# Four small moves in the opening of a fused FFT and SoLU kernel: the mean row of w_out, its last piece, the first down product, and the loads of the second pair

## The chip, the cores, the metric

The kernel runs on one core of a Trainium2 chip. The metric is device time in microseconds (us), the median of several executions. The profile's span (first to last instruction) is some 2 us shorter than the device time of the same execution.

## The reference

```python
# x: (8, 3136, 256); w_in: (256, 1024); w_out: (1024, 256); g_ln: (1024,)
X = np.fft.fft(np.fft.fft(x, axis=1), axis=2).real          # then (25088, 256)
h = X @ w_in
e = np.exp(h - h.max(-1, keepdims=True))
solu = h * e / (e.sum(-1, keepdims=True) + 1e-9)
ln = (solu - solu.mean(-1)) / np.sqrt(solu.var(-1) + 1e-6) * g_ln
out = ln @ w_out
```

## The kernel before

The eight batches are handled as four pairs. A pair's rows are transformed along the sequence in two stages (`transform1`, `transform2`, with a trip through DRAM between them), and each row block of the result is a *unit*: an "up" product with w_in (the feature transform is folded into it), the softmax-like middle, and a "down" product with w_out. Unit 0 has one half, the others two (signs 0 and 1). Subtracting the mean over features is done once, on w_out: its mean row is subtracted (`centre`), and `weight_sums` prepares four differences of blocks for a seven-product multiplication. The weights come as 64-bit floats and are converted by integer operations (`exponent`, `confine`, `narrow`).

```python
def confine(unit, here=False):              # limit the exponent
    if here:                                # two operations on VectorE
        bits(unit, unit, -896.0, ALU.add, 0.0, ALU.max)
        bits(unit, unit, 255.0, ALU.min, 2.0 ** 23, ALU.mult)
        return
    ...                                     # else three on ScalarE
def centre(self):
    cs = result(0)[:, 0:D]
    for c in range(KF):
        nc.tensor.matmul(cs, ones, Wo[:, c, :], start=(c == 0), stop=(c == KF - 1))
    nc.scalar.mul(out=wbar, in_=cs, mul=1.0 / FF)
    nc.vector.tensor_tensor(out=Wo, in0=Wo, in1=wbar.unsqueeze(1).to_broadcast([P, KF, D]), op=ALU.subtract)
def weight_sums():                          # four on GpSimd, each 128x512
    for j, (a, b) in enumerate(((B12, B11), (B22, Ws[:, 0]), (B22, B12), (B21, Ws[:, 1]))):
        nc.gpsimd.tensor_tensor(out=Ws[:, j], in0=a, in1=b, op=ALU.subtract)
def ahead(pr, i):                           # loads, mirror sum (GpSimd), fold (VectorE) of a later pair
    if i == (pr.p - 1) * NK:
        load(pr, 0); load(pr, 1)            # each: one DMA of SyncE, one gather of GpSimd
    ...
# The opening (cuts marked; engines in comments)
...
for i in range(1, 3): weights.narrow_out(i)             # VectorE
for t in units[:2]: take2(t, transform2(...)); spread(t)  # spread: r <- q, 512 bytes
confine(weights.units[-1])                              # ScalarE
for c in (...): keep(first, c, ...)                     # 2.6 MB to DRAM, SyncE's queue
weights.load_table(1)
...
def begin(i):                                           # starts unit i
    enter(i)
    even(cur, up(cur, 0))                               # TensorE, then VectorE: ev = h0 + w_mid * r
    cur.odd = up(cur, 1)
    second_transform(i + 2)                             # TensorE, copied by ScalarE
begin(0)
for i in range(whole + 1):                              # whole = 4
    if prv: turn_whole(prv)                             # TensorE transposes of unit i-1, into four banks
    for s in cur.signs: join(cur, s)                    # VectorE
    if prv: ...                                         # VectorE copies two of the four banks
    for s in cur.signs: expo(cur, s)                    # ScalarE
    if i == whole: ps_o = down(units[0], 0)             # TensorE, 16 matmuls
    if i == 0: weights.narrow_out(3)                    # VectorE
    for s in cur.signs:
        product(cur, s)                                 # VectorE: u = h * u, two SBUF inputs
        if i < whole and s == 0: square(cur, s)         # ScalarE
    if i == 1: weights.centre(); weight_sums()
    if i < whole:
        begin(i + 1)
        if 1 in cur.signs: square(cur, 1)
        stats(cur); power(cur)                          # ScalarE, then GpSimd: rs
    else:
        ...
        scale(units[0], 0, ps_o)
    if i == 0: turn(first, 1, nc.sync)
    other_pairs(i, ahead)
```

Each engine runs its own instructions in the order of the program.

## Time and profile before

| | before |
|---|---|
| median of 6 runs | 1178.57 us (1176.2 to 1179.94) |
| span of the profiled run | 1174.4 us |
| TensorE / VectorE / ScalarE / GpSimd busy | 1132.6 / 1005.7 / 762.4 / 598.2 us |

A row of the timeline gives start, length, engine, source line, operation, the tile written and those read, shapes and count; in brackets, how long the engine idled before it and who ended the wait. A releaser is inferred, so where the engine named had been done for long, another one was meant. The times of the "evens" (line 244, one for each unit) serve as a ruler for the opening; the prediction shows them.

**A measure for what follows.** The code is the same up to the first narrowing of w_out, and from TensorE's first `transform1` of the second pair on. Between them lies all that the diff touches. I call the time from the start of the one to the start of the other *the stretch*: 45.20 to 111.77 us before, so 66.57.

### The profile page before, as it was taken

How to read it: one execution, taken by the hardware profiler on the slowest of the kernel's cores; microseconds unless marked ns; L12 is line 12 of the kernel's file. 1: busy time of each engine (PE TensorE's matmuls, PEld its weight loads, DVE VectorE, ACT ScalarE, POOL GpSimd, SP SyncE). 2: the span in 40 equal slices, each digit the busy share in tenths (PEclk: the TensorE clock that was granted, in tenths of full speed). 3: DMA queues.
4: the chain of work that ended last, by engine and by line, in shares of the span. 5: the costliest groups of instructions: out<-in, count | busy, mean ns of one | idle time of the engine just before them, and what ended most of it. 6: DMA issues, size and time to landing. Idle time of an engine off the chain costs nothing. (4 is left out here: it accounts for less than half of the span.)

```text
span 1174.4 us, 18577 instructions
## 1 busy us (share of the span) xinstructions
PE 1132.6 (96%) x5850; PEld 881.2 (75%) x5850; DVE 1005.7 (86%) x1376; ACT 762.4 (65%) x1841; POOL 598.2 (51%) x558
## 2 busy tenths in 40 slices
PE   2988999999999999999999999999999999999997
PEld 1556787777877787877877777778777787778787
DVE  7789999998878999998879999999887898888870
ACT  4577666757756766767656666676666676677651
POOL 3036666563465566563556666554544334433444
PEclk9999999999999999999999999999999999999999
DMA  9672998865988998865879898865775565745553
GB/s 243 196 186 71 180 183 180 176 141 127 180 185 167 182 167 186 176 141 135 176 146 188 176 188 183 172 146 133 153 154 135 135 152 125 154 108 137 130 116 109
DMA packets 458465, 185.55 MB, mean 158 GB/s; under 512 B 425750, under 2 KB 440350, under 8 KB 458368
## 3 DMA queue, kind: packets, MB, share of 16 engines
q1 hardware_dynamic: 444608, 146.22, 60.4%
q0 software_dynamic: 13760, 38.16, 12.4%
q8 instruction: 47, 0.77, 0.3%
q14 instruction: 50, 0.41, 0.1%
HBM read 44.78 MB, written 38.80 MB: 71 GB/s over the span
## 5 line engine op out<-in xcount | busy, mean ns | idle before, releaser
L443 PE MATMUL ps_m<-Wo,uT 128*128 128x256 f32 x1632 | 369.2, 380 | 3.1 <-ACT uT L321 2.1
L238 PE MATMUL ps_h<-Wi,q 128*128 128x512 f32 x800 | 360.8, 593 | 3.0 <-DVE nmax L252 2.1
L443 PEld LDWEIGHTS ps_m<-Wo,uT 128*128 128x128 f32 x1632 | 314.2, 196 | 33.8 <-ACT uT L321 2.4
L268 DVE SCALAR_TENSOR_TENSOR u<-h,u 128x1024 f32<-128x1024 f32 x196 | 266.1, 1366 | 50.5 <-ACT u L261 36.1
L238 PEld LDWEIGHTS ps_h<-Wi,q 128*128 128x128 f32 x800 | 145.9, 190 | 149.9 <-issue 140.0
L275 ACT ACTIVATE h<-u,usum 128x1024 f32<-128x1024 f32 x196 | 224.4, 1145 | 34.3 <-DVE u L268 33.0
L354 POOL TENSOR_TENSOR S<-uT 128x512 f32<-128x512 f32 x94 | 130.4, 1387 | 208.5 <-issue 138.7
L261 ACT ACTIVATE u<-h,neg 128x1024 f32<-128x1024 f32 x196 | 225.3, 1150 | 6.4
L304 DVE STREAM_TRANSPOSE v<-u 128x1024 f32<-128x1024 f32 x192 | 227.8, 1226 | 0.1
L291 POOL TENSOR_TENSOR rs<-v,neg_half 128x2 f32<-128x2 f32 (+1 forms) x100 | 71.7, 717 | 251.8 <-ACT v L284 251.7
L252 DVE CUSTOM_DVE_ANT_0 h<-ev,ps_h 128x1024 f32<-128x1024 f32 x100 | 122.2, 1222 | 33.3 <-PE ps_h L238 23.5
L244 DVE SCALAR_TENSOR_TENSOR ev<-w_mid,r,ps_h 128x1024 f32<-128x1024 f32 x100 | 126.7, 1267 | 25.6 <-PE ps_h L238 20.6
L359 PE MATMUL ps_m<-Ws,S 128*128 128x128 f32 x1128 | 141.5, 275 | 1.8 <-ACT ot L390 1.8
L216 ACT COPY q<-ps_m 128x256 f32<-128x256 f32 x100 | 36.8, 368 | 159.4 <-PE ps_m L210 155.9
L359 PEld LDWEIGHTS ps_m<-Ws,S 128*128 128x128 f32 x1128 | 133.6, 192 | 2.7 <-issue 1.6
L252 DVE CUSTOM_DVE_ANT_0 h<-h,ps_h 128x1024 f32<-128x1024 f32 x96 | 117.3, 1221 | 13.8
L454 POOL DMA_INDIRECT out_dram<-ot,idx x96 | 100.8, 1050 | 30.7 <-issue 18.7
L359 PE MATMUL ps_m<-Wo,uT 128*128 128x128 f32 x752 | 104.2, 282 | 0.1
L182 PE MATMUL ps_m<-y,F 98*100 98x258 f32 (+3 forms) x288 | 73.4, 390 | 24.7 <-DVE y L130 21.8
L210 PEld LDWEIGHTS ps_m<-T,g 128*128 128x128 f32 x400 | 60.2, 191 | 49.1 <-issue 41.7
L359 PEld LDWEIGHTS ps_m<-Wo,uT 128*128 128x128 f32 x752 | 96.1, 196 | 0.9 <-issue 0.5
L259 ACT ACTIVATE neg<-nmax 128x1 f32<-128x1 f32 x196 | 38.4, 196 | 81.5 <-DVE nmax L252 73.6
(87 smaller groups left out, 1186.7 us busy)
## 6 DMA issues: line engine op xcount, KB each, us to landing
uT<-v SPq DMA_DIRECT2D x752, 128.0 KB
out_dram<-ot SPq DMA_DIRECT2D x100, 128.0 KB
g<-zd POOLq DMA_DIRECT2D x72, 160.0 KB, 5.6
xa<-in_x_dram SPq DMA_DIRECT2D x28, 392.0 KB
zd<-z SPq DMA_DIRECT2D x24, 400.0 KB
raw_in<-in_moe_w_in_dram SPq DMA_DIRECT2D x4, 512.0 KB
raw_out<-in_moe_w_out_dram SPq DMA_DIRECT2D x2, 1024.0 KB
r<-q SPq DMA_DIRECT2D x100, 0.5 KB
```

Source lines behind the costliest of these rows:

```text
L182: nc.tensor.matmul(o[..., cs], F[:, 2 * t + h, :], i[..., cs], start=first, stop=True, skip_group_check=True)
L238: nc.tensor.matmul(ps[:, fs], t.q[:, c * P : (c + 1) * P], Wi[:, c, fs], start=True, stop=True)
L244: nc.vector.scalar_tensor_tensor(out=t.ev, in0=w_mid, scalar=t.r, in1=ps, op0=ALU.mult, op1=ALU.add)
L252: nc.vector.tensor_tensor_reduce(out=t.h[s], in0=t.h[0] if s else t.ev, in1=t.odd, scale=1.0 if s else -0.5, scalar=-3.0e38, op0=ALU.add, ...
L261: nc.scalar.activation(out=t.u[s], in_=t.h[s], func=ACT.Exp, bias=t.neg[:, s : s + 1], accum_out=t.esum[:, s : s + 1])
L268: nc.vector.scalar_tensor_tensor(out=t.u[s], in0=t.h[s], scalar=1.0, in1=t.u[s], op0=ALU.mult, op1=ALU.mult, accum_out=t.usum[:, s : s + 1])
L275: nc.scalar.activation(out=t.h[s], in_=t.u[s], func=ACT.Square, bias=t.usum[:, s : s + 1], scale=-float(FF), accum_out=t.ssq[:, s : s + 1])
L304: nc.vector.transpose(out=t.batch.v[:, t.w, :, o], in_=t.u[s])
L354: nc.gpsimd.tensor_tensor(out=t.S[:, j], in0=a, in1=b, op=op)
L359: nc.tensor.matmul(o, a[:, c], b[:, c], start=start and c == 0, stop=c == n - 1, skip_group_check=True)
L443: nc.tensor.matmul(ps, uT[:, c, :, s], Wo[:, c, :], start=(c == 0), stop=(c == KF - 1))
L454: dma = nc.gpsimd.indirect_dma_start(out=out, out_offset=bass.IndirectOffsetOnAxis(ap=idx[:, i : i + 1], axis=0), in_=t.ot[s], in_offset=None)
```

## The change

It wants VectorE out of the way in the opening, where VectorE sets the pace: the mean row is subtracted by GpSimd; the last piece of w_out is converted together with the others, its exponent confined by GpSimd; the first down product (`down(units[0], 0)`) goes into a gap of TensorE one step sooner; and the loads of the second pair are issued two steps later, out of the way of the small transfer r.

```diff
--- before.py
+++ after.py
@@ -492,13 +492,13 @@
         bits(unit, raw[:, 1 : 2 * NW : 2], 20, ALU.logical_shift_right, 0x7FF, ALU.bitwise_and)
         return unit
 
-    def confine(unit, here=False):
+    def confine(unit, engine=None):
 
         if unit is None:
             return
-        if here:
-            bits(unit, unit, -896.0, ALU.add, 0.0, ALU.max)
-            bits(unit, unit, 255.0, ALU.min, 2.0 ** 23, ALU.mult)
+        if engine:
+            engine.tensor_scalar(out=unit, in0=unit, scalar1=-896.0, scalar2=0.0, op0=ALU.add, op1=ALU.max)
+            engine.tensor_scalar(out=unit, in0=unit, scalar1=255.0, scalar2=2.0 ** 23, op0=ALU.min, op1=ALU.mult)
             return
 
         u = unit.bitcast(FP32)
@@ -606,7 +606,7 @@
             for c in range(KF):
                 nc.tensor.matmul(cs, ones, Wo[:, c, :], start=(c == 0), stop=(c == KF - 1))
             nc.scalar.mul(out=wbar, in_=cs, mul=1.0 / FF)
-            nc.vector.tensor_tensor(out=Wo, in0=Wo, in1=wbar.unsqueeze(1).to_broadcast([P, KF, D]), op=ALU.subtract)
+            nc.gpsimd.tensor_tensor(out=Wo, in0=Wo, in1=wbar.unsqueeze(1).to_broadcast([P, KF, D]), op=ALU.subtract)
 
 
 
@@ -616,7 +616,7 @@
 
     def ahead(pr, i):
 
-        if i == (pr.p - 1) * NK:
+        if i == max((pr.p - 1) * NK, 2):
             load(pr, 0)
             load(pr, 1)
         for c in range(NC):
@@ -701,21 +701,21 @@
         turn(first, 0, nc.sync, 0, 2)
         turn(first, 0, nc.gpsimd, 2, KG)
 
-        confine(weights.units[0], True)
+        confine(weights.units[0], nc.vector)
         for i in range(1, 3):
             confine(weights.units[i])
         weights.product_in(1)
         weights.narrow_out(0)
         weights.exponent_out(3)
+        confine(weights.units[-1], nc.gpsimd)
         weights.product_in(2)
-        for i in range(1, 3):
+        for i in range(1, 4):
             weights.narrow_out(i)
 
         units = [Unit(p, k1) for p in range(NP) for k1 in range(NK)]
         for t in units[:2]:
             take2(t, transform2(pairs[0], t.k1))
             spread(t)
-        confine(weights.units[-1])
         for c in (2, 3, 0, 1, 4, 5, 6, 7):
             keep(first, c, slice(4 * KG, ZR))
         weights.load_table(1)
@@ -739,6 +739,9 @@
             cur = units[i]
             enter(i)
             even(cur, up(cur, 0))
+            if i == whole:
+
+                scale(units[0], 0, down(units[0], 0, result(1)[:, 0:D]))
             cur.odd = up(cur, 1)
             second_transform(i + 2)
 
@@ -761,11 +764,6 @@
                     nc.vector.tensor_copy(out=o, in_=ps)
             for s in cur.signs:
                 expo(cur, s)
-            if i == whole:
-                ps_o = down(units[0], 0)
-            if i == 0:
-
-                weights.narrow_out(3)
             for s in cur.signs:
                 product(cur, s)
                 if i < whole and s == 0:
@@ -786,7 +784,6 @@
                     turn_blocks(cur, s)
                 stats(cur)
                 power(cur)
-                scale(units[0], 0, ps_o)
             if i == 0:
                 turn(first, 1, nc.sync)
             other_pairs(i, ahead)
```

## The prediction

> **What bounds the kernel now.** I began with the page: span 1174.4 us, TensorE 1132.6 us busy, VectorE 1005.7. The table of busy time by stretch (columns: stretch, length, then busy us and, in brackets, instructions of TensorE, weight load, VectorE, ScalarE and GpSimd, granted clock, DMA share, GB/s) tells which engine holds which stage:
>
> ```profile
> 60.00:80.00 20.00, 17.10 (x72) 10.68 (x72) 17.57 (x26) 14.08 (x33) 8.07 (x8) 1.00 0.96 226
> 80.00:100.00 20.00, 16.72 (x75) 10.76 (x74) 19.37 (x29) 18.04 (x42) 5.21 (x6) 1.00 0.12 29
> 120.00:140.00 20.00, 20.00 (x107) 15.86 (x106) 18.50 (x25) 13.72 (x37) 13.08 (x14) 1.00 0.90 166
> 200.00:300.00 100.00, 100.00 (x537) 79.45 (x536) 91.71 (x122) 69.64 (x174) 50.83 (x47) 1.00 0.69 152
> ```
>
> From about 112 us TensorE has no idle worth naming. It does the same work before and after, so the change can pay only by how much sooner that full stretch begins. Before it, VectorE sets the pace: 19.37 of 20 us between 80 and 100. All parts of the diff lie there. The chain of waits that ended last covers the final 3 us and says nothing of it, so I read the timeline of the opening. One step is VectorE's even (L244), two joins (L252), sometimes two PSUM copies (L761), two products (L268). The evens stand at 58.13, 64.73, 75.29, 82.72, 90.20 and 101.22 us. The step from 64.73 to 75.29 is the odd one, 10.6 us where its neighbours take 7.4:
>
> ```profile
> 70.65 1.23 DVE L268 SCALAR_TENSOR_TENSOR u<-h,u 128x1024 f32<-128x1024 f32 x1
> 72.09 2.29 DVE L609 TENSOR_TENSOR Wo<-Wo,wbar 128x2048 f32<-128x2048 f32 x1 [0.21 <-ACT wbar L608]
> 74.47 1.28 POOL L342 TENSOR_TENSOR Ws<-Wo 128x512 f32<-128x512 f32 x1 [4.33 <-DVE Wo L609]
> 75.29 1.28 DVE L244 SCALAR_TENSOR_TENSOR ev<-w_mid,r,ps_h 128x1024 f32<-128x1024 f32 x1 [0.91 <-DMA r<-q]
> 80.44 1.24 DVE L268 SCALAR_TENSOR_TENSOR u<-h,u 128x1024 f32<-128x1024 f32 x1
> 82.72 1.30 DVE L244 SCALAR_TENSOR_TENSOR ev<-w_mid,r,ps_h 128x1024 f32<-128x1024 f32 x1
> ```
>
> See the subtraction (2.29), 0.21 ahead of it for wbar, and 0.91 behind it for a 512-byte transfer, r of unit 2. GpSimd's four weight sums run from 74.47 to 79.5, and the products of unit 2 start only at 80.44, so they miss each other.
>
> **What the Trainium skill says.** "GPSIMD Engine Reference", Performance versus the Vector engine, lists a two-input add of 2048 fp32 columns at 2293 ns on VectorE and 4497 on GpSimd. The trace agrees on VectorE (2.29 us); GpSimd's own points here are 1.28 us for 512 columns and 2.37 for 1020, a slope of 2.15 ns per column, so 2048 columns make 4.6 us (estimate). The same page, Engine selection, calls one-input GpSimd work roughly line-rate; no row here shows one on 512 columns. "SBUF — State Buffer", SBUF: two separate sides, says a VectorE op with two SBUF inputs and a GpSimd op that reads SBUF exclude each other for a whole instruction. The trace agrees: products take 1.23 us alone but, beside GpSimd's S sums in the step at 101 us,
>
> ```profile
> 105.11 1.04 POOL L354 TENSOR_TENSOR S<-uT 128x512 f32<-128x512 f32 x1
> 105.44 1.80 DVE L268 SCALAR_TENSOR_TENSOR u<-h,u 128x1024 f32<-128x1024 f32 x1 [0.17 <-ACT u L261]
> 106.11 2.29 POOL L354 TENSOR_TENSOR S<-uT,S 128x512 f32<-128x512 f32 x1
> 107.17 2.31 DVE L268 SCALAR_TENSOR_TENSOR u<-h,u 128x1024 f32<-128x1024 f32 x1
> ```
>
> they alternate: 1.80 and 2.31. Even and join read one operand from PSUM, and at 74.5 to 79.5 they ran beside the weight sums at 1.28 and 1.22, unharmed. "DMA: Bandwidth & Descriptors", Queues, rings and completion order, says each DMA engine takes a ring in order and alternates between rings. The wait for r fits: it is issued at 68.05 behind large transfers of its own queue, while GpSimd's two x gathers (issued 67.80 and 69.17, some 0.39 MB each) share the engines from another.
>
> **The change, part by part.**
>
> *Last piece of w_out.* ScalarE loses three conversions (3 x 0.72, 56.6 to 58.9), and nothing waited for ScalarE there. VectorE's four-stage narrowing (0.42 + 0.69 + 0.75 + 0.88 = 2.74) moves from 60.94 to 56.05, before the first even. VectorE idled 2.08 us there (the row names ScalarE; the matmuls of h at 56.16 to 58.0 are the real release). So the first even goes from 58.13 to 56.05 + 2.74 = 58.8. The first product comes 4.1 us after it (even 1.28, join 1.22, maximum 0.1, then 1.5 for negation and exponential), at 62.9 instead of 63.59: gain 0.7. Against it: the two new GpSimd ops, some 0.7 each (estimate from the line-rate remark plus dispatch), start near 53 when GpSimd has issued its gather (50.56 to 52.9), beside narrowing ops with two SBUF inputs; lock turns can cost VectorE 0 to 1.4. Net between +0.7 and -0.7; I take 0.
>
> *Mean subtraction.* VectorE loses 2.29 and 0.21, and is ready for the third even at 72.0. GpSimd runs it from 72.2 to 76.8, the weight sums to 81.8. Nothing needs them before the first seven-product step near 101; TensorE's first down product, near 85, needs Wo alone.
>
> *x loads of the second pair, two steps later.* This takes 0.78 MB of gather out of r's way. The transfers queued ahead of r had about 0.48 MB left when the gathers began near 69 (windows of bytes moved: 2.8 MB of 3.28 MB gone). At about 220 GB/s that ends at 71.1 alone and 73.4 shared. r was seen at 75.2, so 1.8 us go to completion: r lands near 72.9 now. The third even thus goes from 75.29 to about 73.0: **gain 2.3**, not the 3.4 of removed VectorE time plus waits, because r takes over as limit. The loads, now issued around 85 to 88, land by 91 to 93; GpSimd's mirror sum stood at 93.25 behind rs, so they stay hidden.
>
> *What is paid back.* The products of unit 2 now start at 73.0 + 5.15 = 78.15, inside the weight sums (76.8 to 81.8). By the alternation above, the first waits out the sum in flight (0.6 to 1.2) and the second a whole one (1.2): **loss 1.2 to 2.4, I take 1.8**. So the fourth even goes from 82.72 to about 82.2.
>
> *First down product.* TensorE's 16 matmuls (3.73 us) leave the place where they waited 2.14 for their bank and push the next up product:
>
> ```profile
> 93.58 3.73 PE L443 MATMUL ps_m<-Wo,uT 128*128 128x256 f32 x16 [2.14 <-ACT uT L321]
> 97.14 3.60 PE L238 MATMUL ps_h<-Wi,q 128*128 128x512 f32 x8
> 108.92 2.02 PE L359 MATMUL ps_m<-Ws,S 128*128 128x128 f32 x16 [0.80 <-ACT ot L390]
> 111.77 1.11 PE L182 MATMUL ps_m<-y,F 98*100 98x258 f32 x4 [0.83 <-ACT q L216]
> ```
>
> TensorE gets about 3 us ahead at 97. But it stops again at 108.9 and 111.8 for ScalarE, which follows VectorE's products, so most of this becomes waiting. In its new place, between the halves of unit 4's up product at 85, it ends near 89 and the second half near 90.7, while the join that reads it starts near 91: a tight fit, no loss expected.
>
> *Sum.* VectorE's chain 0 + 2.3 - 1.8 = 0.5 us sooner, which reaches the end one for one; some 0.5 more if the alternation is milder or TensorE's lead saves one of the two waits.
>
> **The rivals.** (1) *The lock does not bite* and the products keep 1.23 us: gain 2.3 to 3, about 1175. For it: small ordering changes can let VectorE's products pass together. Against: the rows at 105 and 107. (2) *The lock bites at all places*, narrowing and products, and the displaced up product delays the join: 0.5 to 1.5 us slower, about 1179. For it: GpSimd carries 10 us of work between 72 and 82, nearly all of one step. (3) *r is not helped* by moving the loads, being bound by its own queue: the third even stays near 74.5 to 75 and products and sums overlap less; about equal to before. Against: only 0.48 MB stood ahead of it when the gathers came. (4) *TensorE is the bound in the opening too*, and the moved down product pays its 2.14 us in full: about 1175. Against: its 0.80 and 0.83 us of waits after it.
>
> **Range and chances.** The runs before lie between 1176.2 and 1179.94, so the clock itself adds about 1.5 either way. Path gain 0.5 to 1, some weight on rival 1 and 4 (each about 1 in 4) over 2 (1 in 5): predicted 1176.6, range 1173.4 to 1179.6. Two per cent is 23.6 us; all that the change touches on VectorE's path is under 7 us, so leaving the band of 2% needs an accident such as a mistimed load: 1 in 100 each way.
>
> **What would show it.** The third even at about 73.0 with r as its releaser; the subtraction on GpSimd at 4.6 us; the products of unit 2 above 1.23, summing to about 4.2; the fourth even near 82; TensorE waiting longer before 108 and full from about 111. The prediction is wrong if the products stay at 1.23 (then faster), if the third even comes at 72 (r no limit), if GpSimd's subtraction takes well over 4.6 us and runs into the products itself, if the mirror sum waits for the late loads, or if TensorE's stretch after 112 is not as full as its busy share says.

## The result

The changed kernel took 1181.82 us (1180.67 to 1183.5, 6 runs) against 1178.57: ratio 1.003, 95% interval 1.0017 to 1.0043. A ratio is the mean time of one kernel's fast runs over that of the other's of the same rounds, so not quite the ratio of the medians. It is within 2%, as forecast, but slower, and outside the range.

The profiled run has a span of 1181.6 us. Of the 7.2 us over the 1174.4 of before, 3.1 came before the first narrowing, where no instruction differs, and 1.2 after the stretch. The stretch itself went from 66.57 to 69.47 us: **2.90 longer**, which agrees with the 3.25 between the medians. The evens share it out (us from the first narrowing):

| | before | changed | difference |
|---|---|---|---|
| second even | 19.53 | 19.86 | +0.33 |
| third even | 30.09 | 28.33 | -1.76 |
| third to fourth | 7.43 | 9.44 | +2.01 |
| fourth to fifth | 7.48 | 7.45 | -0.03 |
| fifth to sixth | 11.02 | 13.76 | +2.74 |
| sixth to the end of the stretch | 10.55 | 10.49 | -0.06 |
| stretch | 66.57 | 69.47 | +2.90 |

(The stretch is the sum of the rows from the third even down.) The timeline of the changed kernel, first part, shows the GpSimd work and what it does to VectorE:

```profile
58.12 1.96 POOL L501 TENSOR_SCALAR scratch<-scratch 128x512 int32<-128x512 int32 x1
...
75.55 4.56 POOL L609 TENSOR_TENSOR Wo<-Wo,wbar 128x2048 f32<-128x2048 f32 x1 [4.60 <-ACT wbar L608]
...
76.61 1.28 DVE L244 SCALAR_TENSOR_TENSOR ev<-w_mid,r,ps_h 128x1024 f32<-128x1024 f32 x1 [1.31 <-DMA r<-q]
...
82.08 1.83 DVE L268 SCALAR_TENSOR_TENSOR u<-h,u 128x1024 f32<-128x1024 f32 x1 [0.22 <-ACT u L261]
...
82.78 2.26 POOL L342 TENSOR_TENSOR Ws<-Wo 128x512 f32<-128x512 f32 x1
...
83.83 2.29 DVE L268 SCALAR_TENSOR_TENSOR u<-h,u 128x1024 f32<-128x1024 f32 x1
```

The second of the two new confining operations takes 1.96 us (the first 2.04); a narrowing operation beside it (L522, at 58.21) is stretched to 1.10 (0.75 before). The subtraction takes 4.56. The third even comes sooner, held by r as predicted. Then the products of unit 2 take 1.83 and 2.29 us, turn about with the weight sums, which grow to 2.26. Before, these two products took 1.24 us each, at 80.44 and 81.58. The second part holds the surprise:

```profile
86.05 1.27 DVE L244 SCALAR_TENSOR_TENSOR ev<-w_mid,r,ps_h 128x1024 f32<-128x1024 f32 x1
...
86.19 1.97 PE L316 MATMUL ps_m<-ident,u 128*128 128x128 f32 x8 [1.13 <-DVE u L268]
...
87.94 2.71 PE L238 MATMUL ps_h<-Wi,q 128*128 128x512 f32 x4
...
90.49 3.62 PE L443 MATMUL ps_m<-Wo,uT 128*128 128x256 f32 x16
...
93.94 1.88 PE L238 MATMUL ps_h<-Wi,q 128*128 128x512 f32 x4
...
95.95 1.22 DVE L252 CUSTOM_DVE_ANT_0 h<-ev,ps_h 128x1024 f32<-128x1024 f32 x1 [1.17 <-PE ps_h L238]
...
96.30 0.37 ACT L216 COPY q<-ps_m 128x256 f32<-128x256 f32 x1 [1.62 <-PE ps_m L210]
...
97.85 1.22 DVE L252 CUSTOM_DVE_ANT_0 h<-h,ps_h 128x1024 f32<-128x1024 f32 x1 [0.66 <-ACT h L275]
...
100.92 1.81 DVE L268 SCALAR_TENSOR_TENSOR u<-h,u 128x1024 f32<-128x1024 f32 x1 [0.65 <-ACT u L261]
...
114.91 2.02 PE L359 MATMUL ps_m<-Ws,S 128*128 128x128 f32 x16 [0.69 <-ACT ot L390]
```

Read it downward. TensorE's transposes (L316) wait 1.13 for the second, lengthened product, and so does the fourth even; the eight of them take 1.97 us (1.09 in e10, below). The first half of unit 4's up product (L238) takes 2.71 us for four matmuls. The down product (L443) starts only at 90.49, 4.44 us after the fourth even at 86.05, and the second half of the up product stands behind it. So the first join of unit 4 (the L252 at 95.95) waits 1.17 for TensorE. The copy of the next transform (L216 at 96.30) comes late as well, and ScalarE's square behind it; the second join waits 0.66 for that square, because it takes over the buffer that the square uses, and the first product 0.65 for the exponential. In the last row TensorE still stops for ScalarE (0.69, and again 0.82 at 117.75), as before. The 3 us by which TensorE had run ahead became idle time, and the delay of VectorE went to the end.

### The profile page after: what moved, and what is told of

Read it like the earlier page. It is cut to its first block, busy times and chain, and to the rows that moved or that the text cites.

```text
span 1181.6 us, 18579 instructions
## 1 busy us (share of the span) xinstructions
PE 1136.4 (96%) x5850; PEld 884.1 (75%) x5850; DVE 1007.9 (85%) x1375; ACT 760.5 (64%) x1838; POOL 608.9 (52%) x561
## 5 line engine op out<-in xcount | busy, mean ns | idle before, releaser
L443 PE MATMUL ps_m<-Wo,uT 128*128 128x256 f32 x1632 | 369.1, 380 | 0.9 <-ACT q L216 0.9
L238 PE MATMUL ps_h<-Wi,q 128*128 128x512 f32 x800 | 362.3, 595 | 2.2 <-DVE nmax L252 1.1
L443 PEld LDWEIGHTS ps_m<-Wo,uT 128*128 128x128 f32 x1632 | 314.3, 196 | 31.9 <-ACT q L216 1.3
L268 DVE SCALAR_TENSOR_TENSOR u<-h,u 128x1024 f32<-128x1024 f32 x196 | 268.9, 1380 | 52.9 <-ACT u L261 41.8
L238 PEld LDWEIGHTS ps_h<-Wi,q 128*128 128x128 f32 x800 | 146.6, 191 | 149.2 <-issue 139.9
L252 DVE CUSTOM_DVE_ANT_0 h<-ev,ps_h 128x1024 f32<-128x1024 f32 x100 | 122.1, 1221 | 34.8 <-PE ps_h L238 24.3
L216 ACT COPY q<-ps_m 128x256 f32<-128x256 f32 x100 | 36.8, 368 | 163.2 <-PE ps_m L210 159.7
L252 DVE CUSTOM_DVE_ANT_0 h<-h,ps_h 128x1024 f32<-128x1024 f32 x96 | 117.2, 1221 | 14.3 <-ACT h L275 0.7
```

The source lines that it names most:

```text
L238: nc.tensor.matmul(ps[:, fs], t.q[:, c * P : (c + 1) * P], Wi[:, c, fs], start=True, stop=True)
L252: nc.vector.tensor_tensor_reduce(out=t.h[s], in0=t.h[0] if s else t.ev, in1=t.odd, scale=1.0 if s else -0.5, scalar=-3.0e38, op0=ALU.add, ...
L268: nc.vector.scalar_tensor_tensor(out=t.u[s], in0=t.h[s], scalar=1.0, in1=t.u[s], op0=ALU.mult, op1=ALU.mult, accum_out=t.usum[:, s : s + 1])
L443: nc.tensor.matmul(ps, uT[:, c, :, s], Wo[:, c, :], start=(c == 0), stop=(c == KF - 1))
```

## The experiments

All outputs are right. Times of evens are counted from the first narrowing; all columns but the last two are from the one profile of each run. Each ratio is to the runs of the kernel before in the same rounds; their medians were 1177.83 to 1178.95.

| run | third even | 3rd to 4th | 4th to 5th | 5th to 6th | stretch | median, us | ratio to before, 95% |
|---|---|---|---|---|---|---|---|
| before | 30.09 | 7.43 | 7.48 | 11.02 | 66.57 | 1178.57 | |
| changed | 28.33 | 9.44 | 7.45 | 13.76 | 69.47 | 1181.82 | 1.0030 (1.0017 to 1.0043) |
| changed again (e14) | 27.88 | 10.42 | 7.45 | 13.76 | 70.01 | 1180.40 | 1.0021 (1.0011 to 1.0031) |
| e1 down product back | 28.38 | 9.02 | 7.45 | 11.05 | 66.43 | 1179.93 | 1.0011 (0.9994 to 1.0028) |
| e2 down product alone | 29.11 | 7.43 | 8.22 | 12.84 | 68.13 | 1180.34 | 1.0007 (0.9990 to 1.0025) |
| e3 subtraction alone | 29.91 | 8.78 | 7.45 | 11.02 | 67.70 | 1179.01 | 1.0000 (0.9983 to 1.0018) |
| e4 late loads alone | 29.10 | 7.44 | 7.45 | 11.06 | 65.57 | 1177.02 | 0.9986 (0.9968 to 1.0004) |
| e5 last piece alone | 29.36 | 7.45 | 7.45 | 11.01 | 65.81 | 1178.61 | 0.9999 (0.9986 to 1.0013) |
| e6 same, confined by ScalarE | 33.29 | 7.44 | 7.45 | 11.01 | 69.73 | 1181.65 | 1.0032 (1.0021 to 1.0042) |
| e7 changed, sums spaced | 28.76 | 7.46 | 7.73 | 13.42 | 67.88 | 1180.16 | 1.0012 (1.0002 to 1.0021) |
| e10 changed, scaling later | 28.36 | 9.62 | 7.45 | 13.69 | 69.63 | 1181.32 | 1.0027 (1.0018 to 1.0036) |
| e13 changed, sums held back | 28.32 | 7.59 | 7.60 | 12.40 | 66.41 | 1178.37 | 1.0005 (0.9994 to 1.0016) |
| e11 a new version | 26.67 | 9.32 | 7.58 | 12.98 | 67.07 | 1177.89 | 1.0001 (0.9988 to 1.0013) |
| e12 e11 with the down product moved | 26.67 | 9.31 | 7.60 | 12.43 | 66.51 | 1179.32 | 1.0007 (0.9999 to 1.0015) |
| e15 e11, loads one step sooner | 26.70 | 9.32 | 7.58 | 11.01 | 65.13 | 1176.73 | 0.9994 (0.9983 to 1.0004) |
| e17 late loads and down product | 29.10 | 7.44 | 7.45 | 12.46 | 66.95 | 1178.76 | 1.0008 (0.9999 to 1.0017) |

The theory after reading the trace (D): the displaced down product costs the 2.7 us. The main rival (L): the lock between GpSimd and VectorE costs them.

### One part undone, one part alone

e1 puts the down product and its scaling back:

```diff
-            if i == whole:
-                scale(units[0], 0, down(units[0], 0, result(1)[:, 0:D]))      # in begin()
+            if i == whole:
+                ps_o = down(units[0], 0)                                      # behind the exponentials
...
+                scale(units[0], 0, ps_o)                                      # at the end of step 4
```

> The changed kernel with the first down product and its scaling put back to where they were; the other three parts stay. Theory D (the displaced down product costs the time: in the changed kernel's trace the span from the fifth to the sixth even is 13.76 us against 11.02 before): that span returns to 11.0 to 11.3 us and the time falls 2.5 to 3 us below the changed kernel, to within 0.8 us of the kernel before (ratio 0.9995 to 1.0007). Rival L (the shared lock between GpSimd and VectorE, in the narrowing and in the products, costs it): the kernel stays 2.5 us or more slower than before (ratio 1.002 or above).

The span from the fifth to the sixth even returns to 11.05, and the stretch to 66.43, 0.14 less than before. By the trace, D holds for this span. By the median the kernel is within noise of before, so the ratio alone would have decided little.

e2 is the diff's down product alone on the kernel before (the same lines, the other way round).

> The kernel before with the down product moved and nothing else. Theory D: the join of unit 4 waits about 1.2 us for TensorE, the next join and product 0.5 to 0.7 each for ScalarE, the span from the fifth to the sixth even is 13 to 13.8 us, and the time is 2 to 3 us above before (ratio 1.0017 to 1.0026). Rival L: no GpSimd work is added, so the ratio is within 0.0006 of 1. A third view, that the cost needs the other parts' shift of the step, would give something between.

The span is 12.84, somewhat below the 13 expected, and the step ahead of it is 0.74 longer too. TensorE's row of that kernel shows why the second is not the down product's doing:

```profile
84.27 0.68 PE L210 MATMUL ps_m<-T,g 128*128 128x128 f32 x4 [1.74 <-DMA xa<-in_x_dram]
```

The transform at 84.27 waited 1.74 us for gathered rows. (Some releaser names such as `xa` stand for a transfer of the same queue.) So the down product was late here too (at 88.26, 4.35 us after the fourth even at 83.91), but for another reason than in the changed kernel. e2 doesn't separate its place from a late TensorE; e17 was made for that.

e3 and e4 are one line each:

```diff
-            nc.vector.tensor_tensor(out=Wo, in0=Wo, in1=wbar...     # e3
+            nc.gpsimd.tensor_tensor(out=Wo, in0=Wo, in1=wbar...
-        if i == (pr.p - 1) * NK:                                    # e4
+        if i == max((pr.p - 1) * NK, 2):
```

> The kernel before with the mean row subtracted by GpSimd and nothing else. My account: r still lands near 75.2 us, so the third even gains nothing; the subtraction takes 4.5 to 4.6 us, the products of unit 2 collide with one or two of the weight sums and lose 1 to 2 us together; ratio 1.0005 to 1.0017. If removing VectorE work pays by itself, the third even comes 2 us or more sooner and the ratio is 0.9985 or below.

> The kernel before with the loads of the second pair issued two steps later and nothing else. My account: r lands by about 73, before VectorE has done the subtraction, so the 0.9 us wait of the third even goes and nothing else moves; ratio 0.999 to 0.9996. If the late loads hurt (mirror sum waiting for them, then the fold), the step from the fifth to the sixth even grows and the ratio is above 1.

With the subtraction alone, the third even waits 3.23 us for r, so removing 2.29 us from VectorE gained 0.18 there; the products of unit 2 took 1.45 and 2.29, the step grew by 1.35, and the stretch by 1.13, as expected. The ratio (1.0000) is too wide to confirm it. With the late loads alone the wait for r is gone, and the stretch is 1.00 shorter, as expected; the ratio (0.9986) leans that way and isn't clear of 1. Nor is one profile proof: in e2 and e5, with the loads in their old place, the third even didn't wait for r either (29.11 and 29.36).

e5 and e6 convert the last piece of w_out in one go, with the exponent confined by GpSimd or by ScalarE:

```diff
+        confine(weights.units[-1], nc.gpsimd)      # e5; e6: without the engine, so by ScalarE
         weights.product_in(2)
-        for i in range(1, 3):
+        for i in range(1, 4):
             weights.narrow_out(i)
```

> The kernel before with the last piece of w_out converted in one go, its exponent confined by GpSimd, and nothing else. From the trace of the changed kernel: each GpSimd operation takes about 2 us instead of the 0.7 I assumed, VectorE's narrowing beside it is stretched by about 1.2 us, so the first even comes 1.6 us later than before (counted from the first narrowing of w_out) and the first product, because the narrowing is out of the way, only 0.3 to 0.4 later or equal; the stretch from the first narrowing to TensorE's first transform of the second pair stays within 0.5 us of 66.57. Rival: this part hurts by itself, and the stretch is 1 us or more longer.

> As the one before, but the exponent is confined by ScalarE as the other pieces are, so GpSimd does nothing there. If the lock is what stretched the narrowing, the stretched rows return to 0.88, 0.42 and 0.75 us, the first even comes at 58.8 to 59.2 on the clock of before and the first product 0.3 to 0.7 us sooner than before. If the narrowing rows stay long, it was not the lock.

In e5 GpSimd's operations took 2.01 and 1.96 us, the first even came at 14.44 (12.93 before) and the first product 0.25 later. The stretch nevertheless is 0.76 shorter, since the 0.91 wait for r is missing in this profile: r's landing varies from run to run. In e6 the stretched narrowing rows are 0.88, 0.42 and 0.74 again, so it was GpSimd's work beside it, as the lock would have it. But the first product gained only 0.14, and the third even waited 4.23 us for r, which nobody expected; the median is 3.4 us above before, so this is no accident of one profile. In e6 the `keep` transfers ahead of r start 0.9 us later against the first narrowing, while GpSimd's gathers come at the same time (22.5 against 22.6), so more stands ahead of r when the gathers join in. That fits, but no run with e6 and late loads was made, so this cause stays argued.

### The lock, taken out of the changed kernel

e7 spreads the four weight sums out, with one after the subtraction, two after the power of step 2, and one after that of step 3:

```diff
-                weight_sums()
+                weight_sums((0,))
...
                 power(cur)
+                if i in (2, 3):
+                    weight_sums((1, 2) if i == 2 else (3,))
```

> The changed kernel with GpSimd's four weight sums spread out: one right after the subtraction, two after the power of step 2, one after that of step 3, so that they miss the products. If the lock costs the changed kernel its gain in this step, the products of unit 2 return to 1.23 us each, and the span from the third to the fourth even returns from 9.44 to 7.4 to 7.9 us. If the span stays at 9 us or more, the products are not what lengthens it. The down product's cost, by my account, stays: the span from the fifth to the sixth even 12.8 to 13.8 us.

Timeline of e7:

```profile
79.93 1.21 DVE L268 SCALAR_TENSOR_TENSOR u<-h,u 128x1024 f32<-128x1024 f32 x1
...
95.40 2.34 POOL L137 TENSOR_TENSOR xa<-xa,xb 98x1020 f32<-98x1020 f32 x1
...
95.80 3.03 DVE L268 SCALAR_TENSOR_TENSOR u<-h,u 128x1024 f32<-128x1024 f32 x1 [0.62 <-ACT u L261]
```

The products of unit 2 are back at 1.21 and 1.22 (the second at 81.07), and the span from the third to the fourth even at 7.46. The 2.0 us were the lock. In the last two rows the same lock strikes elsewhere: the fourth sum pushes the mirror sum (L137) into the first product of unit 4, which takes 3.03. So the 13.42 of this run can't be charged to the down product.

e13 holds all four sums back behind the products of unit 2, with a tiny GpSimd operation that reads their sums:

```diff
+        gate = small.tile([P, 2], FP32, tag="gate", name="gate", bufs=1)
+        nc.gpsimd.tensor_tensor(out=gate, in0=t.usum, in1=neg_half, op=ALU.mult)    # first in weight_sums(t)
...
                     square(cur, 1)
+                if i == 2:
+                    weight_sums(cur)
                 stats(cur)
```

> The changed kernel with its weight sums held back in the same way and nothing else. The lock as cause of the late TensorE: products of unit 2 at 1.23 us, the span from the third to the fourth even 7.4 to 7.7 us (9.44 in the changed kernel), the transposes of that step no longer wait for the products, the down product begins 3.2 to 3.7 us after the fourth even (4.44), the span from the fifth to the sixth even 11.0 to 12 us (13.76), the stretch 65 to 66.5 us. If the down product costs by its place alone, the span from the fifth to the sixth even stays above 12.8.

The products take 1.21 and 1.23, and the down product begins 3.15 us after the fourth even (85.81 and 82.66) instead of 4.44. The stretch is 66.41. But the span from the fifth to the sixth even is 12.40, above the 11 to 12 that the lock alone would leave. So 1.36 us of the 2.74 left in this run, and 1.38 stayed with the down product's place. That the 1.36 were the lock's doing doesn't follow, for a second thing differs: in the changed kernel the granted clock fell just ahead of the down product, and here it held. e10, next, tells the two apart.

### The down product's place

e10 leaves the down product and moves only its scaling behind ScalarE's second square and statistics:

```diff
-                scale(units[0], 0, down(units[0], 0, result(1)[:, 0:D]))
+                units[0].ps = down(units[0], 0, result(1)[:, 0:D])
...
                 power(cur)
+                if i + 1 == whole:
+                    scale(units[0], 0, units[0].ps)
```

> The changed kernel with the down product where it is, but its scaling on ScalarE put behind the second square and the statistics of that step. If ScalarE's wait for the down product's result (0.48 us in the changed kernel) is what delays the joins, the span from the fifth to the sixth even falls from 13.76 to below 12 us. If TensorE's order does it (the second half of the up product and the next transform stand behind the down product, and ScalarE's copy of that transform stands ahead of its square), at most 0.6 us comes back.

The span is 13.69 against 13.76, but its rows are not those of the changed kernel:

```profile
83.17 1.27 DVE L244 SCALAR_TENSOR_TENSOR ev<-w_mid,r,ps_h 128x1024 f32<-128x1024 f32 x1
...
83.30 1.09 PE L316 MATMUL ps_m<-ident,u 128*128 128x128 f32 x8 [1.13 <-DVE u L268]
...
84.49 1.98 PE L238 MATMUL ps_h<-Wi,q 128*128 128x512 f32 x4
...
86.31 3.62 PE L443 MATMUL ps_m<-Wo,uT 128*128 128x256 f32 x16
...
92.06 1.22 DVE L252 CUSTOM_DVE_ANT_0 h<-ev,ps_h 128x1024 f32<-128x1024 f32 x1 [0.17 <-DVE ev L244]
...
94.75 3.18 PE L316 MATMUL ps_m<-ident,u 128*128 128x128 f32 x16 [2.66 <-ACT ot L448]
```

The lock is all there: the products of unit 2 take 1.83 and 2.29, the span from the third to the fourth even is 9.62, and the transposes wait 1.13 for the second product. But the granted clock held at 1.00, the transposes take 1.09 and the first half of the up product 1.98, and the down product starts 3.14 us after the fourth even, as in e13. So the lengthened products alone don't make it late: the even waits for them too, and the up product waits for the even (its weight load by 0.34 here, by 0.26 before). The first join waits 0.17, and the second comes 1.61 after it, just as in e17 below, where the scaling isn't moved; so ScalarE's wait for the down product's result isn't what delays the joins. The 13.69 has a cause of its own. The moved down product writes a bank (`result(1)`) that the transposes of unit 3 take over; with the scaling late they wait 2.66 for it, and VectorE's copies 2.22 for them.

e17 is the kernel before with the lines of e4 and of e2, the late loads and the moved down product, so neither the lock with the weight sums nor late rows.

> The kernel before with the late loads and the moved down product, nothing else. If the place costs by itself, through ScalarE's copy and square that stand behind the down product, the first join of unit 4 does not wait for TensorE, the second waits 0.2 to 0.7 us, the first product 0.6, and the span from the fifth to the sixth even is 12.2 to 12.6 us (11.02 before, 11.06 with the late loads alone); the stretch is 66.7 to 67.2 us (65.57 with the loads alone). If the place is free when TensorE is on time, the span is below 11.4 us. If the late TensorE had nothing to do with it, the span is 13.4 us or more as in the changed kernel.

```profile
83.80 1.98 PE L238 MATMUL ps_h<-Wi,q 128*128 128x512 f32 x4
...
85.62 3.62 PE L443 MATMUL ps_m<-Wo,uT 128*128 128x256 f32 x16
...
91.37 1.22 DVE L252 CUSTOM_DVE_ANT_0 h<-ev,ps_h 128x1024 f32<-128x1024 f32 x1 [0.17 <-DVE ev L244]
...
92.98 1.22 DVE L252 CUSTOM_DVE_ANT_0 h<-h,ps_h 128x1024 f32<-128x1024 f32 x1 [0.38 <-ACT h L275]
...
96.05 1.80 DVE L268 SCALAR_TENSOR_TENSOR u<-h,u 128x1024 f32<-128x1024 f32 x1 [0.64 <-ACT u L261]
```

The span is 12.46 and the stretch 66.95, both inside what was expected. The first half of the up product takes 1.98 again, the down product starts 3.15 us after the fourth even (82.47), and the first join waits 0.17, no more than usual. The place's own cost is then read off row by row against before. The time from the first join to the second is 1.61 (1.38): the square stands behind the copy of the late transform. The time from the copies to the first product is 1.93 (1.20): the exponential comes late. The time from the first product to the second is 1.73 (1.25): the mirror sum, which waits for rs behind the late statistics, meets the product. That is 0.23 + 0.73 + 0.48 = 1.44, the whole of 12.46 - 11.02. In the changed kernel the same rows give 0.52 + 0.73 + 0.49, and the first join adds 1.00.

### The lowered clock

e14 is the changed kernel once more.

> The changed kernel again, for a second profile: was the lowered TensorE clock between 86 and 90 us (0.55 to 0.6) chance? If it was, it is missing here or elsewhere, the first half of unit 4's up product takes 1.98 us again instead of 2.71, and the span from the fifth to the sixth even falls by about 0.7 us from 13.76; if the clock falls in the same place, it belongs to the change.

The clock fell in the same place again (0.50 and 0.74 from 84 to 88 us), the four matmuls took 2.81, and the span was 13.76. By the words above it would belong to the change. But e10 and e1 are the same program up to the end of these four matmuls, and there the clock held at 1.00 (1.98 us in both). So it fell in two of four profiles. The table of stretches of the changed kernel's first profile (third number from the end: granted clock):

```profile
84.00:86.00 2.00, 1.06 (x8) 0.82 (x8) 2.00 (x1) 1.45 (x3) 2.00 (x2) 1.00 0.00 0
86.00:88.00 2.00, 1.81 (x9) 1.82 (x10) 1.83 (x4) 1.80 (x5) 1.93 (x2) 0.55 0.42 56
88.00:90.00 2.00, 2.00 (x4) 0.81 (x4) 1.86 (x3) 1.97 (x5) 1.61 (x2) 0.60 0.87 283
```

The clock is 0.55 and 0.60 just after TensorE was busy for only 1.06 of 2 us; in e10 it held after 0.87 of 2 us in the same place. Of the 1.29 us by which the down product starts later than in e13 and e17, 0.73 are the slower matmuls (2.71 - 1.98) and 0.55 the later start of the half ahead of it (1.89 after the fourth even, 1.34 in e13), which stands behind the slower transposes (1.97 against 1.09 in e10). So all of it goes with the lowered clock. In e10, e13 and e17 the clock held in this place. All eight profiles with the moved down product show a drop to about 0.5 somewhere between 94 and 112 us, seven of them around the sixth even; it cost nothing there, since the span from the sixth to the seventh even is 10.42 to 10.48 with it and without. But e5, e6 and e15, with the down product in its old place, have drops too, and before shows none after an idle gap of 2.14 us at 91.4. What sets off a drop isn't settled.

### A version that uses what was found

e11 takes the kernel before, the late loads, GpSimd's subtraction and the held-back sums, and loads the table's second half behind r of unit 2:

```diff
-        weights.load_table(1)
...
         begin(0)
+        weights.load_table(1)
```

> The version I would keep: the kernel before with the late loads and GpSimd's subtraction, the down product and the narrowing left as they were, the second half of the table loaded after r of unit 2 instead of ahead of it, and the weight sums held back by one tiny GpSimd operation that reads the products' sums of unit 2. My account: the third even comes at 26.8 to 27.2 us after the first narrowing (30.1 before), products at 1.23 us throughout steps 1 to 3, the stretch from the first narrowing to the first transform of the second pair 63 to 64 us (66.57 before), ratio 0.9968 to 0.998. If the opening is bound by something else, the stretch stays above 65.5.

The third even came at 26.67, so r no longer limits, but the stretch, 67.07, missed the 63 to 64 expected. The next span is 9.32 instead of 7.4: with VectorE that early, the joins and products wait for TensorE (0.53) and ScalarE (0.66 and 0.67), which in the program's order stand behind the column sums of `centre`. (e14, with its third even at 27.88, shows the two waits of 0.66 too, and 10.42.) So an earlier third even is in part given back at once. And the mirror sum met the products of unit 4, because its gathers had slid behind the sums (first profile e11, second e15):

```profile
95.35 2.35 POOL L137 TENSOR_TENSOR xa<-xa,xb 98x1020 f32<-98x1020 f32 x1 [1.90 <-DMA xb<-in_x_dram,idx]
...
95.51 3.28 DVE L268 SCALAR_TENSOR_TENSOR u<-h,u 128x1024 f32<-128x1024 f32 x1
```

```profile
92.20 2.35 POOL L137 TENSOR_TENSOR xa<-xa,xb 98x1020 f32<-98x1020 f32 x1
...
94.33 1.31 DVE L268 SCALAR_TENSOR_TENSOR u<-h,u 128x1024 f32<-128x1024 f32 x1
```

e12 is e11 with the moved down product.

> The kernel above with the down product moved as in the change. If the new place has no slack but no cost of its own while TensorE reaches it in time (as with the spaced sums, where the first join of unit 4 did not wait for it), the span from the fifth to the sixth even is 11.0 to 11.8 us and the ratio is within 0.0006 of that of the kernel above. If the place costs by itself, the span is 12.8 us or more and the ratio is 0.0015 or more higher.

The span is 12.43, between the two expected, so the place is not free, as in e13 and e17. The ratio can't be used as expected, since e11 itself had lost 2 us in this span.

e15 issues the gathers one step sooner than e11:

```diff
-        if i == max((pr.p - 1) * NK, 2):
+        if i == max((pr.p - 1) * NK, 1):
```

> The gated version with the gathers issued at the end of step 1 instead of step 2, ahead of GpSimd's held-back sums. If only the sliding of the mirror sum cost it its gain, the products of unit 4 return to 1.3 us or so (3.28 there), the span from the fifth to the sixth even to 11.0 to 11.4 us (12.98), and the stretch to 64.8 to 65.6 us. The step from the third to the fourth even stays near 9.3 us, because there TensorE and ScalarE, behind the column sums of w_out, set the pace. If the span stays above 12.5, the mirror sum was not it.

The product of unit 4 takes 1.31, the span is 11.01, the stretch 65.13, all as expected: the slid mirror sum was the cause. This stretch is 1.44 us shorter than before's and 4.34 shorter than the changed kernel's. In the median it is 1176.73 against 1177.95 of the same rounds, ratio 0.9994, not clear of 1. It is the shortest stretch found, and clearly ahead of the changed kernel in the stretch, but that it beats the kernel before in time isn't shown.

## Why the prediction was wrong

- **What bounds the opening** (VectorE, until TensorE's full stretch at 112 us): right. The delay of VectorE reached the end one for one, and TensorE's lead turned into waits, as said; rival 4 falls.
- **Last piece of w_out**, taken as 0: the second even came 0.33 later (0.86 in e14). The term that was mis-sized is GpSimd's confining operation: 0.7 us assumed, 1.96 to 2.46 measured. It had no effect beyond, because r held the third even.
- **Mean subtraction**: 4.6 predicted, 4.56 measured.
- **x loads**: r takes over as the limit, as predicted; gain 1.76 for 2.3 (third even at 28.33 for 27.8 after the first narrowing). r's landing varies by more than this miss from run to run.
- **What is paid back**: 2.01 for 1.8, the two products 4.12 together for 4.2. The reading of the lock was right, and e7 and e13 show it.
- **First down product**, "a tight fit, no loss expected": this step failed. It cost 2.74 us in the changed kernel and 1.44 in e17, where TensorE was on time. The check that the prediction made, whether the first join finds its operand, held in e17 (a wait of 0.17). What it missed is the rest of TensorE's order: behind the down product stands the transform whose copy ScalarE must make before its square, statistics and exponentials, and they make up the 1.44. The other 1.30 came with the granted clock, which fell to 0.55 and 0.50 just ahead of the down product in the two profiles of the changed kernel; with no slack left, the join waited for it. Nothing in the profile of before announced that, and what sets it off stays open. The lengthened products that the prediction foresaw don't suffice: e10 and e1 have them, and their clock held.
- **The sum**: 0.5 us sooner predicted, 2.90 longer measured in the stretch. 2.74 of the 3.4 between them is the down product (1.30 of it only with the lowered clock); the rest is 0.5 of gain less and 0.2 of lock more. Rival 2 named the displaced up product and the lock, with 1 chance in 5; its 0.5 to 1.5 us was too small.

## What to carry to other kernels

Before an instruction is moved into a gap of one engine, follow everything behind it in that engine's order to the other engines: here a gap long enough for the matmuls still delayed a copy, and with it a second engine. "Tight fit" is no slack: here 1.3 us of delay ahead of the moved work, from a clock that fell where it had not before, went straight to the engine that sets the pace. Two runs with nearly equal spans (13.76 and 13.69) can have different causes, so compare their rows before reading one as no effect. Work given to GpSimd should be placed by when VectorE has no operation with two SBUF inputs, and the gathers queued behind it on GpSimd need to be followed as well.

## What the Trainium skill lacked or had wrong

- "GPSIMD Engine Reference", Engine selection, calls one-input operations on GpSimd roughly line-rate. A `tensor_scalar` with two operations on 128x512 int32 took 1.96 to 2.46 us in seven profiles (changed, e1, e5, e7, e10, e13, e14), longer than the two-input fp32 operation on 128x512 (1.28). It ran beside VectorE's narrowing, so part of it may be waiting; by how much, no run shows.
- "SBUF — State Buffer", SBUF: two separate sides, says who blocks whom but not who goes next. Here GpSimd and VectorE took strict turns when both had a queue: products of 1.83 and 2.29 us, sums of 2.26 (1.23 and 1.28 alone).
- "TensorE: Matmul & The Clock Gate", HAM oscillation, gives idle gaps over some 3.4 us as the thing to avoid; the section behind it speaks of short idles too, but gives no length for them. In the changed kernel the granted clock fell to 0.55 after gaps of 0.82 and 1.13 us in a stretch where TensorE was about half busy (1.18 and 1.06 of 2 us). It held at 1.00 after gaps of 0.94 and 1.13 in the same place in e10 (1.06 and 0.87 of 2 us), and in the kernel before through a gap of 2.14. So the length of the gaps doesn't decide here.
- "DMA: Bandwidth & Descriptors", Queues, rings and completion order, says how the engines alternate between rings, but gives no figure for what that costs a small transfer. Where GpSimd's gathers ran beside it, the third even, held by r, came at 29.91 and 33.29 us after the first narrowing (e3, e6); where they came later, at 27.88 to 28.36 (changed kernel twice, e10). But in e2 and e5 they ran beside it too, and r was in time for 29.11 and 29.36, so the cost varies.
